# A fused RG-LRU and mixture-of-experts kernel: twelve row tiles for eight, two pairs of PSUM banks for turned tiles, one bank for the second GEMM, and new ranks

## The chip, the cores and the metric

The kernel runs on one core of a Trainium2 chip. The metric is the device time of one execution in microseconds, lower is better. Its engines are TensorE (PE: products; PEld: their weight loads), VectorE (DVE), ScalarE (ACT), GpSimd (POOL) and SyncE (SP), each with its own queue of instructions.

## The reference

A gated linear recurrence runs over four sequences of 5056 tokens with 256 features, and its output goes through a mixture of eight experts, each token to one of them.

```python
log_a = 8.0 * sigmoid(r_gate) * log(clip(sigmoid(a_param), 1e-6, 1 - 1e-6))
a = exp(log_a)
x_gated = sqrt(max(1 - a * a, 1e-6)) * sigmoid(i_gate) * x
for t in range(S):
    h = a[:, t] * h + x_gated[:, t]
    y[:, t] = h
x = y.reshape(20224, 256)
logits = x @ w_gate                           # [N, 8]
e_idx = argmax(logits, axis=1)
gate_w = softmax(logits)[n, e_idx]
eom = sigmoid(x @ w_output_gate)
for e in range(8):
    mask = e_idx == e
    out[mask] = gate_w[mask] * eom[mask, e] * (relu(x[mask] @ w1[e]) @ w2[e])
```

`w1` is [8, 256, 1024], `w2` [8, 1024, 256]. All inputs are float32.

## The kernel before

**Tiles.** The tokens lie along the free axis, features on the partitions. They come in 20 chunks of eight tiles of 128 tokens (the last has six), each chunk in two blocks of 512 tokens. For a block, three loads (L520) bring r, i and x; ScalarE makes tanh, exponential, square and root (L526 to L545), VectorE the gated inputs (L532, L548) and the scan (L579). A block is scaled by a power of two from its maximum (L613, a product on TensorE at L263 that spreads it, L268) and cut into a high and a low half of 16 bits (L627 or L629, L632). Both halves are turned into rows of tokens by products with an identity, which carry the two gates' columns along (L653, "projection", four products of 160 columns into a pair of PSUM banks). ScalarE copies the turned rows into a row tile (L660), VectorE adds the gates' parts up to logits (L664).

**Routing.** When a chunk's eight tiles have logits, VectorE and ScalarE find each token's expert and weight (L673 to L723), TensorE counts places (L694, L696, "ranks"), VectorE makes positions (L727 to L739), and GpSimd scatters the eight row tiles to a table in memory sorted by expert (L354). From chunk 2 on, a scatter also waits for the newest ReLU, so that scatters are spread in time. VectorE then plans slots (L790 to L821): a slot is a run of 256 (early and late in the kernel 128) rows of one expert.

**Slots.** For a slot, SP fetches its rows turned (L868) and the expert's w1 in two halves (L894). GEMM1 (L921) makes hidden units in groups of 512 columns in three PSUM banks; ScalarE's ReLU (L936) and VectorE's rest (L939) split each into two halves of 16 bits. GEMM2 (L965) sums over them, three products for each of eight slices, into one PSUM bank; ScalarE scales it to a result (L977) and GpSimd scatters that to the output (L980). Three slots at the very end run only if they hold rows.

**Weights.** Each of 16 units (eight of w1, eight of w2) is loaded as float32 (L408) into the place of the unit after next, or for the last two into buffers of the slots that chunk 1 has used. A Gram product (L434) and its square (L440) give a power of two, with which it is split (L471 or L473, L481). No slot's weights are fetched before all of w1 is split, no GEMM2 runs before all of w2 is.

**Order.** The program lists all steps as `work(engine, time, emit, after, rank, ...)`, and `in_order` turns the list into one order for each engine: it steps through a modelled time, and each engine that comes free takes, of the steps whose predecessors are done in the model, the one with the least rank. `UNIT_RANK`, `CHUNK_RANK` and `SLOT_RANK` rank units, chunks and the slots of early chunks; later chunks have 2 + c, later slots -5 + s/1000. `TAIL` is added for a chunk's steps from L613 to L664, `ROOT` for its roots, `QUICK` for routing; `EARLY` ranks the projections and ranks on TensorE; `UNIT_LOAD`, `CHUNK_LOAD` and `LOAD_RANK` rank the loads on SP. GEMM2 of a slot has the slot's rank plus `LAG`, GEMM1 the slot's rank plus f/10000 for slice f. The engines then run their instructions in that order, each waiting on semaphores for what it needs.

A `Ring(n)` says in the model when a buffer comes free: a new use waits for the use n before it. The tile pools behind the rings make the same wait on the chip. Of the eight PSUM banks, GEMM1 has three (`ps_h`), GEMM2 and the Gram products two (`ps_o`), projections one pair (`ps_t`), and norms and ranks one (`ps_r`). `rt`, `it` and `xt` hold blocks of r, i and x; a block's buffer of x is in use from its load to its last projection.

Of the kernel before, what the change touches and what calls it, by code (L numbers as in the profile page):

```python
# [7 lines left out]
F32 = mybir.dt.float32  # L8
F16 = mybir.dt.float16
# [3 lines left out]
ALU = mybir.AluOpType  # L13
# [4 lines left out]
P = 128  # L18
# [17 lines left out]
XT = 3  # L36
ROWS = 8
# [4 lines left out]
LAG = 0.05099  # L42
ALONE = (0, 1, 2, 3, 4, 5, 6, 7)
QUICK = 38.13505
ROOT = 275.35116
EARLY = -3648.57348
UNIT_RANK = (56.129, -3501.769, -3458.728, -978.998, -58.723, 38.307, 48.956, 15.508, -257.769, 37.957, -138.469, -385.108, -20.771, -510.085, 59.783, -1.802)
CHUNK_RANK = (-854.714, -3616.617, -3494.371, -1109.025, -778.437, -192.081)
SLOT_RANK = (-1097.603, -1306.253, -459.569, 1089.226)
LOAD_RANK = -3488.5456  # L50
STAGED = {14: ('hh', 'hh'), 15: ('hh', 'ws')}
WINDOW, WARM = 3.413, (0.8, 0.35)
UNIT_LOAD = (244.464, 345.534, 1294.322, -3524.389, -3500.663, -1010.087, 280.646, 98.454, 33.972, -3596.229, 186.523, 60.803, 179.63, -3596.513, -253.138, 1086.46)
CHUNK_LOAD = (84.95, 1021.338, 257.343, 30.647, 1292.223, 0.423)
TAIL = -440.29839
TOPS = 2
TABLES = -854.61171
DEPTH = 3
SLACK = (0.022, 0.414)
# [110 lines left out]
def rglru_moe(ctx: ExitStack, tc: tile.TileContext, x, r_gate, i_gate, a_param, wg, wog, w1, w2, out, shape):  # L170
    nc = tc.nc
    D, N = x.shape
    B, S = shape
    E, _, F = w1.shape
# [6 lines left out]
    while sum(n for _, n in chunks) < NT:  # L181
        t = sum(n for _, n in chunks)
# [29 lines left out]
    ps_o = ctx.enter_context(tc.tile_pool(name="ps_o", bufs=2, space=bass.MemoryType.PSUM))  # L212
    ps_t = ctx.enter_context(tc.tile_pool(name="ps_t", bufs=1, space=bass.MemoryType.PSUM))
    ps_r = ctx.enter_context(tc.tile_pool(name="ps_r", bufs=1, space=bass.MemoryType.PSUM))
# [138 lines left out]
    def scatter_rows(pos, rows, c):  # L353
# [17 lines left out]
        "mt": Ring(6), "ot": Ring(2), "osc": Ring(4), "plan": Ring(3), "ps_h": Ring(3), "ps_o": Ring(2), "am": Ring(4), "ps_t": Ring(1), "ps_r": Ring(1),  # L371
    }
    tiles = {}
# [12 lines left out]
    def unit(u, staged):  # L386
# [10 lines left out]
        m = size // g  # L397
# [27 lines left out]
        pg, old = rings["ps_o"].new()  # L425

        def gram():
            t = tiles["pg", u] = ps_o.tile([P, 512], F32, name=f"pg_{u}", tag="ps_o")
            k = 0
            for fw in fws:  # L430
                upper = fw.bitcast(BF16).rearrange("p (n two) -> p n two", two=2)
                for f in range(0, m, P):
                    blk = upper[:, f:f + P, 1]
                    nc.tensor.matmul(t[:, 0:P], lhsT=blk, rhs=blk, start=k == 0, stop=k == size // P - 1)  # L434
                    k += 1

        def square():
            dg = small.tile([P, P], F32, name=f"dg_{u}", tag="dg", bufs=1)
            sq = tiles["sq", u] = small.tile([P, 1], F32, name=f"sq_{u}", tag="sq")
            nc.scalar.activation(dg, tiles["pg", u][:, 0:P], AF.Square, accum_out=sq)  # L440

        def total():
            nc.tensor.matmul(tiles["pg", u][:, P:P + 1], lhsT=ones32, rhs=tiles["sq", u], start=True, stop=True)
# [53 lines left out]
    def chunk(c):  # L497
# [100 lines left out]
        for b in range(0, nt, 4):  # L598
# [38 lines left out]
            pu, pold = rings["ps_r"].new()  # L637
# [5 lines left out]
            for j in range(b, b + nb):  # L643
# [24 lines left out]
                lows.append(work("DVE", 0.22, lz, [w] + chain["small"], front, uses=[pu]))  # L668
# [76 lines left out]
        pu, pold = rings["ps_r"].new()  # L745
# [26 lines left out]
    def plan(group):  # L772
# [15 lines left out]
        def emit():  # L788
# [4 lines left out]
            nc.vector.tensor_tensor_scan(bound[:, 1:E + 1], ones32[:, 0:E], own, 0.0, op0=ALU.mult, op1=ALU.add)  # L793
# [50 lines left out]
    def slot(s):  # L844
# [63 lines left out]
        for f0 in range(0, NF, per):  # L908
# [33 lines left out]
            m = work("ACT", 0.57, relu, [m, hold], rank, uses=[pu, hu])  # L942
            evac.append(work("DVE", 0.66, low, [m], rank, uses=[pu, hu]))
# [69 lines left out]
    pu, pold = rings["ps_r"].new()  # L1013
# [75 lines left out]
```

## Time and profile before

| | us |
|---|---|
| median of three runs | 1109.23 (1108.28 to 1113.5) |
| the profiled execution | 1111.95 |
| its span, first to last instruction | 1110.3 |
| TensorE busy in the span | 982.2 (88%) |
| VectorE busy | 713.0 (64%) |
| ScalarE busy | 693.4 (62%) |
| GpSimd busy | 354.9 (32%) |
| mean granted clock of TensorE | 0.969 |

Busy time is the union of an engine's instructions. Matmuls are pipelined and overlap, so a busy TensorE is not one at its peak: its work is better counted as products times the distance of their starts. "Idle <- X" means that the engine stood before an instruction and that X ended the wait.

### The profile page before, as it was taken

What the parts mean: (1) busy time and instruction counts of PE and PEld (TensorE: products, weight loads), DVE (VectorE), ACT (ScalarE), POOL (GpSimd) and SP (SyncE); (2) the same over time, 40 slices, a digit from 0 to 9 for tenths busy, and PEclk for the clock granted to TensorE, in tenths of its full rate; (3) what the DMA queues carried; (4) which work ended last, traced back from release to release, by engine and by line L of the source; (5) the groups of instructions that cost most, each with busy time, mean ns of one, the idle gap of its engine ahead of it and who ended that gap; (6) DMA issues with size and microseconds to landing.
All of it is one profiled execution on the core that took longest, in us unless ns stands there. A gap on an engine that the chain in (4) does not pass through costs nothing.

```text
span 1110.3 us, 29698 instructions
## 1 busy us (share of the span) xinstructions
PE 982.2 (88%) x9820; PEld 866.6 (78%) x9820; DVE 713.0 (64%) x1729; ACT 693.4 (62%) x1105; POOL 354.9 (32%) x346
## 2 busy tenths in 40 slices
PE   1355489989999999999989999999999999999997
PEld 1344488878888888788878878888888888888996
DVE  7899878678868667575765657576675753333222
ACT  8995746877786667667666766766676442322222
POOL 1013344243343423324332332433333344312111
PEclk9966599999999999999999999999999999999999
DMA  9972699998867777685968768586875646657782
GB/s 347 387 247 68 215 302 285 300 288 271 248 230 216 234 236 202 211 244 189 239 202 239 199 213 225 208 210 218 258 193 197 192 155 193 173 158 222 240 246 87
DMA packets 196862, 249.42 MB, mean 225 GB/s; under 512 B 120013, under 2 KB 128976, under 8 KB 196720
## 3 DMA queue, kind: packets, MB, share of 16 engines
q1 hardware_dynamic: 180928, 204.17, 62.6%
q0 software_dynamic: 15792, 43.31, 11.7%
q8 instruction: 95, 1.56, 0.6%
q14 instruction: 47, 0.39, 0.1%
HBM read 79.09 MB, written 43.81 MB: 111 GB/s over the span
## 4 chain that ended last, share of the span: by engine, by line
PE 46%; issue 21%; DMA 13%; ACT 8%; DVE 6%; POOL 5%; SPq 1%; POOLq 0%; ACTq 0%; DVEq 0%
PE po L965 21%; PE ph L921 21%; DMA xs<-rows_all,posi 7%; DMA xt<-xs 3%; POOL out_dram L980 3%; PE pt L653 3%; POOL xs L354 2%; ACT rows_all L660 2%; DVE it L579 1%; DMA rt<-in_r_gate_dram 1%; ACT w1r L471 1%; DVE w2r L481 1%; ACT it L540 1%; DMA it<-in_i_gate_dram 1%; ACT it L545 1%
## 5 line engine op out<-in xcount | busy, mean ns | idle before, releaser
L965 PE MATMUL po<-w2r,h 128*128 x3888 | 486.4, 272 | 10.7 <-issue 4.8
L921 PE MATMUL ph<-xt,ws 128*128 128x256 f16 (+1 forms) x4752 | 471.4, 255 | 10.7 <-DMA xt<-xs 5.6
L921 PEld LDWEIGHTS <-ws 128*128 128x128 f16 x4752 | 399.7, 99 | 49.1 <-issue 10.2
L965 PEld LDWEIGHTS <-h 128*128 128x128 f16 x3888 | 373.7, 98 | 72.4 <-issue 16.5
L939 DVE SCALAR_TENSOR_TENSOR h<-ph,h 128x512 f16<-128x512 f32 x324 | 215.0, 684 | 169.0 <-ACT h L936 166.1
L980 POOL DMA_INDIRECT out_dram<-ot,mt x162 | 172.5, 1065 | 386.8 <-ACT ot L977 347.6
L354 POOL DMA_INDIRECT xs<-rows_all,posi x158 | 170.2, 1077 | 352.2 <-issue 159.6
L936 ACT ACTIVATE h<-ph 128x512 f16<-128x512 f32 x324 | 186.1, 599 | 147.9 <-PE po L965 89.2
L660 ACT ACTIVATE rows_all<-pt 128x512 f16<-128x512 f32 x158 | 93.7, 593 | 100.0 <-DMA xs<-rows_all,posi 57.2
L977 ACT ACTIVATE ot<-po,osc 128x256 f32<-128x256 f32 x162 | 70.8, 473 | 121.6 <-PE po L965 104.7
L653 PE MATMUL pt<-iw,xt 128*128 128x160 f16 x632 | 74.8, 243 | 57.6 <-DVE lz L664 33.9
L664 DVE TENSOR_REDUCE lz<-pt 128x16 f32<-128x64 f32 x158 | 35.1, 222 | 122.7 <-PE pt L653 75.6
L653 PEld LDWEIGHTS <-xt 128*128 128x128 f16 x632 | 55.7, 103 | 68.5 <-issue 59.2
L579 DVE TENSOR_TENSOR_SCAN it<-rt,last,it 128x512 f32<-128x512 f32 (+4 forms) x78 | 95.4, 1240 | 0.7
L548 DVE SCALAR_TENSOR_TENSOR it<-it,xt 128x1024 f32<-128x1024 f32 (+1 forms) x40 | 48.3, 1208 | 31.9 <-ACT it L545 31.8
L536 ACT ACTIVATE rt<-rt,lam 128x512 f32<-128x512 f32 (+1 forms) x80 | 61.0, 801 | 0.5
L532 DVE SCALAR_TENSOR_TENSOR xt<-it,xt 128x1024 f32<-128x1024 f32 (+1 forms) x40 | 48.3, 1207 | 6.0 <-ACT it L529 3.2
L632 DVE SCALAR_TENSOR_TENSOR xt<-it,sc,xt 128x1024 f16<-128x1024 f32 (+1 forms) x40 | 49.7, 1265 | 0.3
L613 DVE TENSOR_REDUCE am<-it 128x1 f32<-128x1024 f32 (+1 forms) x40 | 47.8, 1196 | 0.0
L545 ACT ACTIVATE it<-it,quarter 128x1024 f32<-128x1024 f32 (+1 forms) x40 | 45.5, 1138 | 0.4
L529 ACT ACTIVATE it<-it 128x1024 f32<-128x1024 f32 (+1 forms) x40 | 41.6, 1039 | 4.0 <-DMA it<-in_i_gate_dram 3.9
L627 ACT ACTIVATE xt<-it,sc 128x1024 f16<-128x1024 f32 (+1 forms) x36 | 39.8, 1139 | 6.7 <-DVE sc L269 6.7
(146 smaller groups left out, 567.0 us busy)
## 6 DMA issues: line engine op xcount, KB each, us to landing
ws<-w1r SPq DMA_DIRECT2D x198, 512.0 KB
rt<-in_r_gate_dram SPq DMA_DIRECT2D x39, 512.0 KB
it<-in_i_gate_dram SPq DMA_DIRECT2D x39, 512.0 KB
xt<-in_x_dram SPq DMA_DIRECT2D x39, 512.0 KB
w2r<-in_moe_w_dram SPq DMA_DIRECT2D x8, 1024.0 KB
w1r<-in_moe_w_dram SPq DMA_DIRECT2D x6, 1024.0 KB
out_dram<-ot,mt POOLq DMA_INDIRECT x162
xs<-rows_all,posi POOLq DMA_INDIRECT x158
```

The lines of the kernel that those rows point to most:

```text
L354: op = nc.gpsimd.indirect_dma_start(out=xs[:, :], out_offset=bass.IndirectOffsetOnAxis(ap=pos, axis=0), in_=rows.bitcast(F32), in_offset=None,
L536: nc.scalar.activation(r[:, h], r[:, h], AF.Exp, scale=lam[:, h:h + 1], bias=lam[:, h:h + 1])
L545: nc.scalar.activation(t("it"), t("it"), AF.Sqrt, scale=-0.25, bias=quarter)
L579: nc.vector.tensor_tensor_scan(H[:, h, lo:hi], A[:, h, lo:hi], H[:, h, lo:hi], first, op0=ALU.mult, op1=ALU.add)
L653: nc.tensor.matmul(pt[:, k, h * P:h * P + PIECE], lhsT=halves()[:, k, h, (j % 4) * P:(j % 4 + 1) * P], rhs=iw[:, h, :], start=h == 0, stop ...
L660: nc.scalar.activation(rows_all[:, row_at[j], 0:META].rearrange("p (k h d) -> p k h d", k=2, h=ND), src, AF.Copy)
L921: nc.tensor.matmul(ph[:, i], lhsT=ws[:, f // 2 % 2, a, c, f % 2 * P:(f % 2 + 1) * P], rhs=xt[:, b * ND + c, 0:w], start=k == 0, stop=k == ...
L936: newest["relu"] = nc.scalar.activation(part(0, f0), tiles["ph", s, f0], AF.Relu).ins
L939: nc.vector.scalar_tensor_tensor(part(1, f0), tiles["ph", s, f0], 0.0, part(0, f0), op0=ALU.max, op1=ALU.subtract)
L965: nc.tensor.matmul(po[0:pw, j], lhsT=hh[:, a, f % 4, j * P:j * P + pw], rhs=w2r[:, bass.ds(eo + (b * NF + f) * D, D)], start=f + j + a + b ...
L977: nc.scalar.activation(ot[0:pw], tiles["po", s][0:pw, j], AF.Copy, scale=tiles["osc", s][0:pw, j, :])
L980: op = nc.gpsimd.indirect_dma_start(out=out[:, :], out_offset=bass.IndirectOffsetOnAxis(ap=tiles["mt", s][0:pw, j, 1:2].bitcast(I32), axis=0),
```

## The change

Buffers. The ring of row tiles (`rows_all`) has 12 tiles instead of 8. The pool `ps_t` has two pairs of banks instead of one, and norms and ranks use it too, so `ps_r` is gone. `ps_o` has one bank instead of two, and the Gram products use the three banks of `ps_h`. The blocks of gated x (`xt`) have two buffers instead of three. Room for the row tiles comes from these, from `ones16` and `ones32`, which shrink to a column and to eight columns and are broadcast where they are used, and from the dump of the Gram's square, which goes into its own PSUM bank.

Order. All ranks are new, and the modelled times of the logits reduction, ReLU and its rest are smaller. `LAG` goes from 0.051 to 0.001.

```diff
-XT = 3
-ROWS = 8
+XT = 2
+ROWS = 12
...
-LAG = 0.05099
+LAG = 0.00109
...
-QUICK = 38.13505
-ROOT = 275.35116
-EARLY = -3648.57348
-UNIT_RANK = (56.129, -3501.769, -3458.728, -978.998, -58.723, 38.307, 48.956, 15.508, -257.769, 37.957, -138.469, -385.108, -20.771, -510.085, 59.783, -1.802)
-CHUNK_RANK = (-854.714, -3616.617, -3494.371, -1109.025, -778.437, -192.081)
-SLOT_RANK = (-1097.603, -1306.253, -459.569, 1089.226)
-LOAD_RANK = -3488.5456
+QUICK = -11.91443
+ROOT = 992.65936
+EARLY = -2725.80744
+UNIT_RANK = (67.516, 56.172, -366.254, -506.545, 5.629, -24.414, 1010.034, 862.588, -2331.179, -2787.321, 491.753, -2254.652, -778.82, 159.232, -593.189, -2302.865)
+CHUNK_RANK = (-2962.244, -191.208, 477.716, 958.712, 983.504, 13.905)
+SLOT_RANK = (969.557, -4.083, -663.468, -155.487)
+LOAD_RANK = 104.33083
...
-UNIT_LOAD = (244.464, 345.534, 1294.322, -3524.389, -3500.663, -1010.087, 280.646, 98.454, 33.972, -3596.229, 186.523, 60.803, 179.63, -3596.513, -253.138, 1086.46)
-CHUNK_LOAD = (84.95, 1021.338, 257.343, 30.647, 1292.223, 0.423)
-TAIL = -440.29839
+UNIT_LOAD = (239.968, 854.707, -9.185, -227.515, -70.138, 130.966, -238.61, 298.25, -2689.191, 13.907, 336.076, -163.291, 56.472, 348.489, -155.228, 298.416)
+CHUNK_LOAD = (-76.123, 359.624, 952.522, -66.657, -13.306, -105.965)
+TAIL = -2745.68701
...
-TABLES = -854.61171
+TABLES = -315.468
...
-SLACK = (0.022, 0.414)
+SLACK = (0.589, 0.209)
...
-    ps_o = ctx.enter_context(tc.tile_pool(name="ps_o", bufs=2, space=bass.MemoryType.PSUM))
-    ps_t = ctx.enter_context(tc.tile_pool(name="ps_t", bufs=1, space=bass.MemoryType.PSUM))
-    ps_r = ctx.enter_context(tc.tile_pool(name="ps_r", bufs=1, space=bass.MemoryType.PSUM))
+    ps_o = ctx.enter_context(tc.tile_pool(name="ps_o", bufs=1, space=bass.MemoryType.PSUM))
+    ps_t = ctx.enter_context(tc.tile_pool(name="ps_t", bufs=2, space=bass.MemoryType.PSUM))
...
-    ones16 = const.tile([P, P], F16, name="ones16")
+    ones16 = const.tile([P, 1], F16, name="ones16")
...
-    ones32 = const.tile([P, P], F32, name="ones32")
+    ones32 = const.tile([P, E], F32, name="ones32")
...
-        pg, old = rings["ps_o"].new()
+        pg, old = rings["ps_h"].new()
...
-            dg = small.tile([P, P], F32, name=f"dg_{u}", tag="dg", bufs=1)
+            dg = tiles["pg", u][:, 2 * P:3 * P]
...
-                tiles["norm", key] = ps_r.tile([P, 512], F32, name=f"norm_{key[0]}_{key[1]}", tag="ps_r")
+                tiles["norm", key] = ps_t.tile([P, 2, 512], F32, name=f"norm_{key[0]}_{key[1]}", tag="ps_t")[:, 0]
...
-                lows.append(work("DVE", 0.22, lz, [w] + chain["small"], front, uses=[pu]))
+                lows.append(work("DVE", 0.16, lz, [w] + chain["small"], front, uses=[pu]))
...
-            pk = tiles["pk", c] = ps_r.tile([P, 512], F32, name=f"pk_{c}", tag="ps_r")
+            pk = tiles["pk", c] = ps_t.tile([P, 2, 512], F32, name=f"pk_{c}", tag="ps_t")[:, 0]
...
-            m = work("ACT", 0.57, relu, [m, hold], rank, uses=[pu, hu])
-            evac.append(work("DVE", 0.66, low, [m], rank, uses=[pu, hu]))
+            m = work("ACT", 0.48, relu, [m, hold], rank, uses=[pu, hu])
+            evac.append(work("DVE", 0.6, low, [m], rank, uses=[pu, hu]))
```

## Rows read from the trace of the kernel before

**Rows 1.** Windows by stage, from the first GEMM1 to the end. Columns: the stretch, its length, then busy us (number of instructions) of PE, PEld, DVE, ACT and POOL, the granted clock of TensorE, the busy share of the DMA engines, GB/s.

```profile
128.00:250.00 122.00, 110.36 (x1361) 99.03 (x1361) 92.74 (x224) 89.21 (x135) 43.81 (x39) 0.95 1.01 285
250.00:300.00 50.00, 48.68 (x463) 42.56 (x462) 40.85 (x94) 38.29 (x63) 17.84 (x16) 1.00 0.87 260
300.00:890.00 590.00, 559.95 (x5233) 490.16 (x5231) 399.00 (x981) 397.12 (x637) 205.53 (x197) 1.00 0.74 217
890.00:1011.00 121.00, 121.00 (x1186) 107.29 (x1185) 47.10 (x147) 37.91 (x78) 42.81 (x44) 1.00 0.59 174
1011.00:1111.00 100.00, 91.33 (x1180) 83.12 (x1177) 24.85 (x50) 26.49 (x51) 17.72 (x18) 0.98 0.64 198
```

**Rows 2.** Windows of the front, the same columns: two of its three stretches, and the sum of the three (0 to 128 us).

```profile
50.00:100.00 50.00, 28.03 (x249) 25.49 (x248) 46.20 (x90) 44.26 (x71) 12.07 (x8) 0.75 0.62 203
100.00:128.00 28.00, 8.40 (x55) 6.51 (x56) 23.99 (x62) 14.31 (x22) 10.62 (x8) 0.50 0.46 156
sum 128.00, PE 50.85 PEld 44.40 DVE 108.42 ACT 104.34 POOL 27.20; mean PE 16.95 PEld 14.80 DVE 36.14 ACT 34.78 POOL 9.07
```

**Rows 3.** The timelines of TensorE and of ScalarE from 918 to 945 us. Columns: start us, duration us, engine, line, operation, written <- read, how many in a row, and in brackets the idle time before and what ended it. TensorE first.

```profile
920.24 5.40 PE L965 MATMUL po<-w2r,h 128*128 x48
925.48 5.40 PE L921 MATMUL ph<-xt,ws 128*128 128x256 f16 x48
930.72 6.98 PE L965 MATMUL po<-w2r,h 128*128 x60
...
933.59 0.84 ACT L977 ACTIVATE ot<-po,osc 128x256 f32<-128x256 f32 x2 [6.00 <-PE po L965]
```

**Rows 4.** TensorE's groups of instructions by line from 300 to 900 us. Columns: line, operation, names, shapes, how many | busy us, mean ns of one | idle us before them in all, and what ended it.

```profile
L965 PE MATMUL po<-w2r,h 128*128 x2369 | 295.5, 272 | 2.6 <-issue 1.9
L921 PE MATMUL ph<-xt,ws 128*128 128x256 f16 x2398 | 286.8, 272 | 6.4 <-DMA xt<-xs 5.6 <-DVE h L939 0.8
L653 PE MATMUL pt<-iw,xt 128*128 128x160 f16 x404 | 44.3, 232 | 21.0 <-ACT rows_all L660 11.3 <-DVE lz L664 9.7
```

**Rows 5.** What ScalarE waited for from 300 to 900 us, the first row: line <- releaser: us in total, times, longest us.

```profile
ACT rows_all L660 <- DMA xs<-rows_all,posi: 57.2, 30, 3.5
```

**Rows 6.** The timeline of all engines at one chunk's projections, from 556 us on.

```profile
556.22 0.44 PE L653 MATMUL pt<-iw,xt 128*128 128x160 f16 x4 [0.74 <-DVE lz L664]
...
559.59 0.60 ACT L660 ACTIVATE rows_all<-pt 128x512 f16<-128x512 f32 x1 [2.74 <-DMA xs<-rows_all,posi]
...
560.24 0.44 PE L653 MATMUL pt<-iw,xt 128*128 128x160 f16 x4 [1.62 <-ACT rows_all L660]
...
560.71 0.22 DVE L664 TENSOR_REDUCE lz<-pt 128x16 f32<-128x64 f32 x1 [2.60 <-PE pt L653]
```

**Rows 7.** The timelines of GpSimd (575 to 640 us) and ScalarE (583 to 616 us): a scatter of one chunk's rows, and a copy of the next chunk's.

```profile
600.16 1.18 POOL L354 DMA_INDIRECT xs<-rows_all,posi  x1 [0.31 <-issue]
...
605.97 0.60 ACT L660 ACTIVATE rows_all<-pt 128x512 f16<-128x512 f32 x1 [3.34 <-DMA xs<-rows_all,posi]
```

**Rows 8.** The chain that ended last, in order of time, from 575 to 640 us: start us, duration us, what.

```profile
623.81 0.29 PE pt L653 x4
624.12 0.38 SPq L520
...
625.22 6.64 DMA xt<-xs
...
631.99 1.59 PE ph L921 x14
```

**Rows 9.** What SP's queue waited for: the row of the x, r and i loads from 300 to 890 us, then a row of the weight loads over the whole span.

```profile
SPq L520 <- PE pt L653: 55.3, 22, 6.3
...
SPq L408 <- PE pt L653: 12.9, 1, 12.9
```

**Rows 10.** The costliest groups by line of the whole span (the columns of rows 4).

```profile
L579 DVE TENSOR_TENSOR_SCAN it<-rt,last,it 128x512 f32<-128x512 f32 (+4 forms) x78 | 95.4, 1240 | 0.7
...
L532 DVE SCALAR_TENSOR_TENSOR xt<-it,xt 128x1024 f32<-128x1024 f32 (+1 forms) x40 | 48.3, 1207 | 6.0 <-ACT it L529 3.2
L632 DVE SCALAR_TENSOR_TENSOR xt<-it,sc,xt 128x1024 f16<-128x1024 f32 (+1 forms) x40 | 49.7, 1265 | 0.3
...
L545 ACT ACTIVATE it<-it,quarter 128x1024 f32<-128x1024 f32 (+1 forms) x40 | 45.5, 1138 | 0.4
```

**Rows 11.** The timeline of ScalarE in the tail, where slots have 128 rows: one result.

```profile
1059.76 0.47 ACT L977 ACTIVATE ot<-po,osc 128x256 f32<-128x256 f32 x1 [0.71 <-PE po L965]
```

**Rows 12.** TensorE's groups by line with the shapes kept apart: GEMM1.

```profile
L921 PE MATMUL ph<-xt,ws 128*128 128x256 f16 x3024 | 358.5, 272 | 7.2 <-DMA xt<-xs 5.6 <-DVE h L939 1.6
L921 PE MATMUL ph<-xt,ws 128*128 128x128 f16 x1728 | 113.0, 224 | 3.5 <-DMA ws<-w1r 3.2 <-DVE h L939 0.2
```

**Rows 13.** The timelines of TensorE and VectorE at the end of the front: the first products of the slots, and the last split of a weight.

```profile
128.73 0.84 PE L921 MATMUL ph<-xt,ws 128*128 128x128 f16 x6
...
136.98 1.36 PE L965 MATMUL po<-w2r,h 128*128 x9 [1.07 <-ACT h L936]
...
132.32 1.28 DVE L481 SCALAR_TENSOR_TENSOR w2r<-fw,wsc,w2r 128x1024 f16<-128x1024 f32 x1
```

**Rows 14.** The timeline of TensorE's weight loads (PEld) at 10 and 18 us: two with a broadcast operand, two with the full `ones`.

```profile
10.23 0.50 PEld L263 LDWEIGHTS norm_gates<-am_gates 128*128 128x128 f32 x2 [10.23 <-DVE am_gates L993]
...
18.81 0.50 PEld L443 LDWEIGHTS pg<-sq,ones 128*128 128x128 f32 x2 [1.94 <-ACT dg L440]
```

More of the change, by code (lines that the diff above doesn't have):

```diff
@@ L370, in rglru_moe @@
         "rt": Ring(RT), "it": Ring(IT), "xt": Ring(XT), "rows": Ring(ROWS), "ws": Ring(3), "hh": Ring(3), "xt16": Ring(3),
-        "mt": Ring(6), "ot": Ring(2), "osc": Ring(4), "plan": Ring(3), "ps_h": Ring(3), "ps_o": Ring(2), "am": Ring(4), "ps_t": Ring(1), "ps_r": Ring(1),
+        "mt": Ring(6), "ot": Ring(2), "osc": Ring(4), "plan": Ring(3), "ps_h": Ring(3), "ps_o": Ring(1), "am": Ring(4), "ps_t": Ring(2),
     }
@@ L422, in unit @@
         loaded[u] = loads
-        pg, old = rings["ps_o"].new()
+        pg, old = rings["ps_h"].new()
         def gram():
-            t = tiles["pg", u] = ps_o.tile([P, 512], F32, name=f"pg_{u}", tag="ps_o")
+            t = tiles["pg", u] = ps_h.tile([P, 512], F32, name=f"pg_{u}", tag="ps_h")
             k = 0
@@ L442, in total @@
         def total():
-            nc.tensor.matmul(tiles["pg", u][:, P:P + 1], lhsT=ones32, rhs=tiles["sq", u], start=True, stop=True)
+            nc.tensor.matmul(tiles["pg", u][:, P:P + 1], lhsT=ones32[:, 0:1].to_broadcast([P, P]), rhs=tiles["sq", u], start=True, stop=True)
         def bits():
@@ L636, in chunk @@
             w = work("DVE", 0.07 + 1.07 * scale, top, [states[b // 4], aold], front, uses=[iu, au])
-            pu, pold = rings["ps_r"].new()
+            pu, pold = rings["ps_t"].new()
             w = work("PE", 0.15, norm, [w, pold], EARLY + c / 100, uses=[pu, au])
@@ L696, in ranks @@
                 nc.tensor.matmul(
-                    pk[:, k * E:(nt + 1) * E], lhsT=ones16, rhs=o2[:, 0:(nt + 1 - k) * E],
+                    pk[:, k * E:(nt + 1) * E], lhsT=ones16.to_broadcast([P, P]), rhs=o2[:, 0:(nt + 1 - k) * E],
                     start=False, stop=k == nt, skip_group_check=True,
@@ L744, in chunk @@
         cn = work("DVE", 0.9, chosen, [ch, ex], quick)
-        pu, pold = rings["ps_r"].new()
+        pu, pold = rings["ps_t"].new()
         pk = work("PE", 0.35, ranks, [cn, pold], EARLY + c / 100, uses=[pu], slack=SLACK[c > 3])
@@ L792, in emit @@
             nc.vector.tensor_copy(own, li)
-            nc.vector.tensor_tensor_scan(bound[:, 1:E + 1], ones32[:, 0:E], own, 0.0, op0=ALU.mult, op1=ALU.add)
+            nc.vector.tensor_tensor_scan(bound[:, 1:E + 1], ones32, own, 0.0, op0=ALU.mult, op1=ALU.add)
             past, o = tile_of("plt", [GROUP, E + 1])[:, 0:n], tile_of("plo", [GROUP, E], bufs=3)[:, 0:n]
@@ L995, in gate_norm @@
     def gate_norm():
-        tiles["norm", "gates"] = ps_r.tile([P, 512], F32, name="norm_gates", tag="ps_r")
+        tiles["norm", "gates"] = ps_t.tile([P, 2, 512], F32, name="norm_gates", tag="ps_t")[:, 0]
         norm_of(tiles["am", "gates"], "gates")
@@ L1012, in rglru_moe @@
     ld = work("DVE", 4.2, log_decay, [lp], -20)
-    pu, pold = rings["ps_r"].new()
+    pu, pold = rings["ps_t"].new()
     au, aold = rings["am"].new()
```

## The prediction

> **What bounds the kernel now.** I read the windows by stage first [rows 1]. From 128 us to the end TensorE is the bound: 110.4 of 122 us busy, then 48.7 of 50, 560.0 of 590, 121.0 of 121 and 91.3 of 100, with VectorE and ScalarE at 25 to 82%. Before 128 us it is not: TensorE is 50.9 us busy of 128, VectorE 108.4, ScalarE 104.3 [rows 2]. So a saving counts in the front only if the first expert products come earlier, and behind it only if TensorE stands still less.
>
> How dense is TensorE really? In the stretch of nothing but products, 48 of them take 5.24 us from start to start in both GEMMs [rows 3], 0.109 us each at 256 columns. From 300 to 900 us there are 2398 + 2369 of them [rows 4], 520 us; 404 products of projections, of 160 columns, are 28 us at the same rate. Ranks and norms I put at 12. That makes 560 us of work in 600, so 40 us is the most that can be won there. Visible idle time is less, 30.1 us from 300 to 890 [rows 1], because busy spans overlap.
>
> Next the idle time of TensorE from 300 to 900 us by line [rows 4]: 11.3 us of projections (L653) for the ScalarE copy out of their PSUM pair (L660), 9.7 us of projections for the logits reduction (L664), 5.6 us of GEMM1 for gathered rows; the three groups have 30.0 us in all. So 21.0 of 30 us belong to the one pair of banks. Behind it the row copies stood 57.2 us for scatters of earlier rows [rows 5]. The timeline shows the chain: a copy begins at 559.59 after 2.74 us of waiting for a scatter's landing, and the projection behind it begins at 560.24 after 1.62 us of waiting for that copy [rows 6]. One ring of eight row tiles makes a chunk's copy wait for the previous chunk's scatters; one pair makes TensorE wait for the copy.
>
> **The change, part by part.** The sum is made against the profiled execution, 1111.95 us (span 1110.3 and 1.65 around it); the median of the three runs is 2.7 below it.
>
> (1) Two pairs and twelve rows. Projection j then waits for the evacuation of j-2, not j-1. A copy needs 0.60 us and a reduction 0.22, and the two projections stand 4.0 us apart [rows 6], so a free pair should be ready. With twelve row tiles the first four copies of a chunk need none of the previous chunk's scatters, which stand now: a scatter of one chunk begins at 600.16, and a copy of the next chunk, after 3.34 us of waiting for such a landing, at 605.97 [rows 7]. Norms and ranks now take turns in the same two pairs, so some projection will still wait for a DVE read of a norm. Between 0 and -21.0 us; I take -18, near the upper end, since each of these waits [rows 4] names a buffer that the change doubles.
>
> (2) Gathered rows. The chain shows why they are late: a projection ends at 624.1, an x load that waited for its buffer follows on SP, and only behind that is the fetch of a slot issued, whose transpose lands 6.64 us later, at 631.9, where GEMM1 starts [rows 8]. SP's x, r and i loads stood 55.3 us for projections [rows 9]. LOAD_RANK turns from far ahead of the slots (-3488) to behind them (+104), so from chunk 6 on a ready fetch is issued ahead of a load: up to -5.6 us. Against it, XT=2 lets an x load start only after the projection two blocks back, not three; queued behind it on SP are fetches (L868) and weight copies (L894), for which TensorE waits. How late is that? A block's buffer goes through its load (6.6, taken as the fetch of [rows 8]), the gated input (1.2), square and root (1.1 each), the second input (1.2), two scans (2.5), the maximum (1.2), norm and scale (1), the two halves (1.1 and 1.3) and four projections, some 2.5 us apart (10): about 28 us, an estimate from [rows 6, 10], where operations without a row are taken as the nearest of their size. 404 products are 12.6 chunks of 32 in 600 us, 47.5 us for each, so some 20 us of cover are left, and no stall by the mean. Between -5.6 and +20; I take -2.
>
> (3) One bank for GEMM2. Today the next slot's products follow at once in the other bank: the row at 930.72 holds 60 products, and a slot's two results are read at 933.59 for 0.84 us in its middle [rows 3]; 24 products from 930.72 are done by 933.3. With one bank the next product starts after 934.4 at the earliest, 1.2 us later, unless TensorE has something else. For a slot of 128 rows the result takes 0.47 us [rows 11], some 0.75 with its start. The forms give 3024/48 = 63 slots of 256 and 1728/48 = 36 of 128 [rows 12]: 63 x 1.2 + 36 x 0.75 = 103 us if nothing covers it, 0 if all is. The cover is one GEMM1 group of a later slot, 12 x 0.109 = 1.31 us (at 128 rows 24 products of half the width, the same). LAG going from 0.051 to 0.001 ranks GEMM2 of slot s only level with GEMM1 of slot s+1, so GEMM1 no longer runs as far ahead of it as its buffers allow, and the planner knows the ring of one. A group is a little longer than the wait, but where ScalarE is inside an activation of 1.14 us [rows 10] the result comes later. I take a twentieth, +5; ends 0 and +103. From 890 to 1011 us TensorE has no idle time to lose [rows 1], so all of it there would be new.
>
> The trace analysis page of the Trainium skill (Perfetto Trace Analysis, Optimizing Tensor Performance) says that independent groups of products should rotate through banks, so that one is read out while the next is computed. For part (1) the trace agrees, 21.0 us of waits with one pair. For GEMM2 the rule speaks against this change; taken alone it would give the 103 us, and the median would be about 1190.
>
> (4) The front. Units and chunks change their order. Gram products of the weights, the splits and two chunks must be done before slots flow: the first GEMM1 starts at 128.73, the first GEMM2 at 136.98 and the last split at 132.32 [rows 13]. Chunk 2's work (rank -3494 before, 477 now) stood ahead of all units but one. On VectorE it is two blocks of 3 x 1.21 (two inputs and the maximum), two scans of 1.24 and a half of 1.27 [rows 10], 14.8 us, that can now come after some splits. But the last loads of weights were themselves late: they need the buffers of chunk 1, and SP stood 12.9 us for one of its projections [rows 9], and chunk 1 (-3616 before, -191 now) falls behind eight units. Units 6 and 7 of w1, without which no slot starts, come last (1010, 862). Grams move to three GEMM1 banks, which are idle then. The granted clock is 0.75 and 0.50 of 2.4 GHz in the last two stretches of the front [rows 2] and full behind [rows 1]; a front that keeps TensorE busier or less busy shifts that by a few us. Between -15 and +15; I take -3, for VectorE's 19.6 idle us [rows 2] leave room.
>
> (5) The rest. `ones` as broadcast operands: a broadcast weight load already stands in the trace, 0.50 us for two, the same as the full one [rows 14]; 32 and 158 loads, 0. The square's dump into PSUM instead of SBUF, 16 short activations in the front: between -1 and +1, taken as 0. The end: the last two slots have no GEMM1 to put between, so +1.
>
> Sum: -18 - 2 + 5 - 3 + 1 = -17, so 1095 us for a profiled execution and 1092 for the median.
>
> **Rivals.** A, the GEMM2 bank decides (slower). Place: every slot change, above all 890 to 1111 us. Price 103 us times the uncovered share; at a fifth it eats the gain, at two fifths it gives -22 + 41 = +19, 1128 for the median. For it: [rows 3, 11], no idle time today. Against: a GEMM1 group is longer than the read-out. The skill's rule above is this rival; how far the trace bears it out is the wait itself, not its cover.
>
> B, XT=2 chokes SP (slower). Place: x loads L520 with fetches behind them. If each of some 15 chunks pays a third of a landing of 6.64 us, 2.2 us, that is +33 and the gain of (2) is gone: about 1127. For it: the chain of [rows 8] and 55.3 us of SP waits [rows 9]. Against: 20 us of cover.
>
> C, the stall only changes its name. The chain in [rows 7, 8], scatter to landing to copy, or fetch to landing, may recur with each chunk; if it and not the banks sets the pace, GEMM1 waits where projections did, and the time is 1109 +- 5. Against: at 890 us, where the projections are nearly over, 221 us of products remain, so routing is well ahead at the end.
>
> D, all parts win: projections' waits and gathered rows -26, the front -15, no bank wait: 1068.
>
> **How the numbers follow.** Forecast 1082 to 1103.6 (0.50), D (0.12), C (0.15), A (0.14), B (0.09). The predicted time is 1092. What a measurement can tell from no change is about 0.5%, 5.5 us. Faster by more: forecast and D, 0.62. Within: C and a little of A and B, 0.16. Slower: A and B, 0.22. The range 1070 to 1120 leaves out the far half of A and B and a little beyond D.
>
> **What would show it.** (1) right: TensorE's waits at L653 from 300 to 900 us fall under 5 us and ScalarE's at L660 for scatters under 20. (2): GEMM1 waits for gathered rows stay under 6 us. (3) right: waits of L965 for L977 under 10 us in all; A: over 25. (4): first GEMM2 between 122 and 152 us. C: L653's waits fall, L921's for gathered rows rise by as much. I am wrong if TensorE's idle time after 300 us is not smaller than the 38.7 us of now (30.0 and 8.7, [rows 1]).

## The result, and the profile after

The changed kernel takes 1079.64 us (median of four runs, 1072.69 to 1080.02) against 1108.76 for the kernel before in the same set: a ratio of 0.9717, 95% interval 0.9667 to 0.9768. A second set gave 0.9705 (0.9683 to 0.9726). The forecast was 1092, so sign and range were right and the gain was 29 us where I had 17; the median lies below the stretch of the forecast (1082 to 1103.6) and above rival D (1068). The profiled execution took 1080.02 us (span 1078.3), 31.9 less than the one of before. Line numbers of the new kernel are one lower: L652 is the projection, L659 the row copy, L663 the logits, L920 GEMM1, L964 GEMM2, L976 the result. Runs made from the kernel before keep its numbers.

First the windows by stage of the changed kernel, columns as in [rows 1].

```profile
128.00:250.00 122.00, 109.98 (x1367) 97.99 (x1365) 95.82 (x244) 88.52 (x140) 47.78 (x40) 0.96 1.01 290
250.00:300.00 50.00, 47.30 (x435) 41.51 (x433) 40.06 (x101) 38.20 (x59) 19.77 (x18) 0.97 0.85 245
300.00:890.00 590.00, 583.26 (x5499) 515.96 (x5497) 412.10 (x1020) 404.15 (x656) 238.94 (x217) 1.00 0.74 228
890.00:1011.00 121.00, 121.00 (x1297) 109.79 (x1295) 41.03 (x110) 36.81 (x70) 23.61 (x24) 1.00 0.56 178
1011.00:1111.00 100.00, 61.27 (x807) 56.83 (x804) 17.18 (x35) 17.77 (x35) 12.78 (x13) 0.98 0.39 132
```

TensorE stands still for 6.7 us from 300 to 890 us, 30.1 before; in the two stretches ahead of that, 14.7 where it was 13.0. Now its groups by line from 300 to 900 us, the same view as [rows 4].

```profile
L964 PE MATMUL po<-w2r,h 128*128 x2507 | 334.8, 272 | 3.4 <-ACT ot L976 2.9
L920 PE MATMUL ph<-xt,ws 128*128 128x256 f16 x2508 | 329.2, 272 | 0.0
L652 PE MATMUL pt<-iw,xt 128*128 128x160 f16 x408 | 38.4, 232 | 2.3 <-ACT rows_all L659 1.3 <-DVE lz L663 0.9
```

The counts say more than the busy time, since spans overlap: 2507 + 2508 products against 2369 + 2398, 248 more in the same 600 us. At 0.109 us each [rows 3] that is 27.0 of the 32.0 us by which the span shrank. At 300 us the two kernels are level: the view by line from 0 to 300 us, with GEMM1's shapes kept apart, has the same 816 narrow products in both, and 582 + 224 wide ones against 576 + 233. The last 5 us came after 900 us; 2.0 of them are visible idle time of the last stretch (99.3 - 91.33 before, 67.3 - 61.27 now), of the rest I have no account.

What TensorE waited for over the whole span, line <- releaser: us in total, times, longest us; the bank of GEMM2 first in the fence, then the two projection waits that [rows 4] showed.

```profile
PE po L964 <- ACT ot L976: 7.3, 12, 1.6
PE pt L652 <- DVE lz L663: 6.0, 2, 5.1
...
PE pt L652 <- ACT rows_all L659: 3.3, 7, 1.5
```

ScalarE's copies no longer wait for any scatter between 300 and 900 us (57.2 us in [rows 5]).

How the one bank of GEMM2 is covered shows in the timelines around one change of slots, first TensorE, then ScalarE (columns as in [rows 3]).

```profile
900.27 0.82 PE L920 MATMUL ph<-xt,ws 128*128 128x256 f16 x6
900.93 0.82 PE L964 MATMUL po<-w2r,h 128*128 x6
901.59 1.47 PE L920 MATMUL ph<-xt,ws 128*128 128x256 f16 x12
902.89 1.55 PE L964 MATMUL po<-w2r,h 128*128 x12
```

```profile
901.84 0.84 ACT L976 ACTIVATE ot<-po,osc 128x256 f32<-128x256 f32 x2
```

GEMM2 of one slot ends with the six products of 900.93. ScalarE reads the result from 901.84 to 902.68, and TensorE has twelve products of GEMM1 in that time, so the next slot's GEMM2 starts at 902.89 without waiting. In the kernel before, 48 products of one GEMM stood in a row [rows 3]; now GEMM1 and GEMM2 alternate by sixes.

Last, VectorE's timeline where a chunk's last logits (`lz`, L663) are made, routing starts (`mx`, L672) and positions are ready (`posi`, L733). The changed kernel first, then the kernel before (L664, L673, L734).

```profile
587.23 0.22 DVE L663 TENSOR_REDUCE lz<-pt 128x16 f32<-128x64 f32 x1 [0.30 <-PE pt L652]
587.48 0.22 DVE L672 TENSOR_REDUCE mx<-lz 128x8 f32<-128x64 f32 x1
...
594.10 0.22 DVE L733 TENSOR_REDUCE posi<-pos 128x8 int32<-128x64 f32 x1
```

```profile
574.84 0.22 DVE L664 TENSOR_REDUCE lz<-pt 128x16 f32<-128x64 f32 x1
...
585.24 0.21 DVE L673 TENSOR_REDUCE mx<-lz 128x8 f32<-128x64 f32 x1
...
593.68 0.22 DVE L734 TENSOR_REDUCE posi<-pos 128x8 int32<-128x64 f32 x1
```

In these rows of before, routing begins 10.4 us after the last logits and the positions come 18.8 us after them; in those of after 0.25 and 6.9. The other chunks go the same way: over chunks 7 to 18, a chunk's first scatter begins 18.5 us after its last logits in the median before, and 8.3 after. The rank that speaks of this is `QUICK`: 2 + c + 38 ranked routing of chunk c behind the gating and the scans of every chunk, 2 + c - 11.9 ranks it ahead of them and, from chunk 6 on, behind the steps of the slots (-5 + s/1000). My prediction has no term for it.

### The profile page after: what moved, and what is told of

It is laid out like the page before. It is cut to its first block, busy times and chain, and to the rows that moved or that the text cites. A ratio compares the mean times of both kernels' runs of the same rounds, so it can differ in the third digit from the quotient of the medians.

```text
span 1078.3 us, 29704 instructions
## 1 busy us (share of the span) xinstructions
PE 972.3 (90%) x9820; PEld 866.3 (80%) x9820; DVE 715.3 (66%) x1743; ACT 687.5 (64%) x1101; POOL 372.8 (35%) x346
## 4 chain that ended last, share of the span: by engine, by line
PE 54%; DMA 8%; ACT 8%; issue 7%; DVE 7%; POOL 3%; SPq 2%; POOLq 0%; ACTq 0%; DVEq 0%
PE po L964 27%; PE ph L920 25%; DMA xt<-in_x_dram 3%; POOL xs L353 2%; PE pt L652 2%; ACT rows_all L659 2%; DMA ws<-w1r 1%; DVE h L938 1%; ACT h L935 1%; DMA rt<-in_r_gate_dram 1%; POOL out_dram L979 1%; DMA xs<-rows_all,posi 1%; DVE it L578 1%; SPq L867 1%; ACT ot L976 1%
## 5 line engine op out<-in xcount | busy, mean ns | idle before, releaser
L964 PE MATMUL po<-w2r,h 128*128 x3888 | 534.0, 273 | 11.5 <-ACT ot L976 7.3
L920 PE MATMUL ph<-xt,ws 128*128 128x256 f16 (+1 forms) x4752 | 528.2, 255 | 15.6 <-DMA xt<-xs 9.2
L920 PEld LDWEIGHTS <-ws 128*128 128x128 f16 x4752 | 409.6, 99 | 56.2 <-issue 12.6
L964 PEld LDWEIGHTS <-h 128*128 128x128 f16 x3888 | 372.2, 98 | 64.6 <-issue 12.9
L935 ACT ACTIVATE h<-ph 128x512 f16<-128x512 f32 x324 | 190.7, 597 | 292.2 <-PE ph L920 287.1
L938 DVE SCALAR_TENSOR_TENSOR h<-ph,h 128x512 f16<-128x512 f32 x324 | 219.7, 686 | 222.4 <-ACT h L935 222.0
L353 POOL DMA_INDIRECT xs<-rows_all,posi x158 | 185.8, 1176 | 311.3 <-ACT h L935 134.3
L659 ACT ACTIVATE rows_all<-pt 128x512 f16<-128x512 f32 x158 | 88.3, 595 | 31.5 <-PE pt L652 16.6
L652 PE MATMUL pt<-iw,xt 128*128 128x160 f16 x632 | 66.0, 243 | 22.3 <-ACT xt L626 8.9
L976 ACT ACTIVATE ot<-po,osc 128x256 f32<-128x256 f32 x162 | 69.8, 470 | 8.0 <-PE po L964 4.9
L652 PEld LDWEIGHTS <-xt 128*128 128x128 f16 x632 | 51.6, 102 | 27.5 <-issue 11.6
L531 DVE SCALAR_TENSOR_TENSOR xt<-it,xt 128x1024 f32<-128x1024 f32 (+1 forms) x40 | 48.3, 1209 | 16.2 <-DMA xt<-in_x_dram 12.8
L663 DVE TENSOR_REDUCE lz<-pt 128x16 f32<-128x64 f32 x158 | 31.6, 220 | 40.7 <-ACT rows_all L659 27.7
L525 ACT ACTIVATE rt<-rt 128x1024 f32<-128x1024 f32 (+1 forms) x40 | 41.8, 1046 | 13.5 <-DMA rt<-in_r_gate_dram 13.3
L539 ACT ACTIVATE it<-rt 128x1024 f32<-128x1024 f32 (+1 forms) x40 | 41.8, 1045 | 8.7 <-DVE xt L531 7.0
```

Of the source, the lines that this page charges most:

```text
L353: op = nc.gpsimd.indirect_dma_start(out=xs[:, :], out_offset=bass.IndirectOffsetOnAxis(ap=pos, axis=0), in_=rows.bitcast(F32), in_offset=None,
L652: nc.tensor.matmul(pt[:, k, h * P:h * P + PIECE], lhsT=halves()[:, k, h, (j % 4) * P:(j % 4 + 1) * P], rhs=iw[:, h, :], start=h == 0, stop ...
L659: nc.scalar.activation(rows_all[:, row_at[j], 0:META].rearrange("p (k h d) -> p k h d", k=2, h=ND), src, AF.Copy)
L920: nc.tensor.matmul(ph[:, i], lhsT=ws[:, f // 2 % 2, a, c, f % 2 * P:(f % 2 + 1) * P], rhs=xt[:, b * ND + c, 0:w], start=k == 0, stop=k == ...
L935: newest["relu"] = nc.scalar.activation(part(0, f0), tiles["ph", s, f0], AF.Relu).ins
L938: nc.vector.scalar_tensor_tensor(part(1, f0), tiles["ph", s, f0], 0.0, part(0, f0), op0=ALU.max, op1=ALU.subtract)
```

## The experiments

Theory 1 is the prediction's: the waits of [rows 4, 5] go because buffers are doubled. Theory 2 says that they go because routing starts at once, so that row tiles are given back early. Each ratio is to the kernel before, run beside it on the same chip, with its 95% interval. From set to set that kernel's median lay between 1108.76 and 1121.72 us, so ratios are compared here, not times.

**All new ranks, old buffers.** The kernel before with every rank, `LAG`, `SLACK` and modelled time of the changed one.

```diff
-LAG = 0.05099
+LAG = 0.00109
...
-QUICK = 38.13505
+QUICK = -11.91443
...
```

> The kernel before with all new ranks, LAG, SLACK and modelled times, but its old buffers (8 row tiles, one pair of banks for projections, two banks for GEMM2, three blocks of gated x). Theory 1, the buffers make the gain: 1098 to 1112 us, TensorE's waits at the projection line from 300 to 900 us stay over 12 us. Theory 2, the order makes the gain: 1076 to 1090 us, those waits under 8 us.

Measured: 0.9914 (0.9881 to 0.9946). From 300 to 900 us the projections wait 8.4 + 3.4 us instead of 21.0, and the copies 3.4 us for scatters instead of 57.2. So the order alone takes off nearly half of the first and nearly all of the second; as a ratio to 1108.76 us, the time is in theory 1's range (0.990 to 1.003), and the waits lie between the marks of the two, 12 and 8 us. But the new order needs the second pair in the beginning, as the windows show:

```profile
250.00:300.00 50.00, 38.33 (x340) 32.98 (x340) 38.17 (x92) 40.36 (x60) 16.53 (x16) 0.83 0.72 212
```

TensorE has 38.3 of 50 us there, 48.7 in [rows 1]. Its timeline has projections one after the other on the single pair, with no GEMM between them:

```profile
252.05 0.69 PE L653 MATMUL pt<-iw,xt 128*128 128x160 f16 x4 [3.96 <-ACT rows_all L660]
255.94 0.69 PE L653 MATMUL pt<-iw,xt 128*128 128x160 f16 x4 [3.20 <-ACT rows_all L660]
```

**New buffers, old ranks.** The reverse: the changed kernel with the ranks, `LAG`, `SLACK` and modelled times of before.

```diff
-LAG = 0.00109
+LAG = 0.05099
...
-QUICK = -11.91443
+QUICK = 38.13505
...
```

> The changed kernel with all old ranks, LAG, SLACK and modelled times, and its new buffers. Theory 1 (buffers): 1076 to 1092 us, waits of TensorE at the projection line from 300 to 900 us under 6 us. Theory 2 (order): 1098 to 1112 us. Rival A on the single GEMM2 bank: with LAG 0.051 the waits of GEMM2 for its result copies rise over 15 us.

Measured: 1.0718 (1.0684 to 1.0753), 1202 us, slower than either theory allowed. GEMM2 waits 54.2 us for its bank over the whole span (rival A's mark was 15), and from 128 to 250 us TensorE is busy for 78.7 of 122 us, 110.4 before. Under an order made for other buffers the new ones cost time, above all the one bank. What the longer ring and the second pair are worth under the old order, this run can't tell.

**Eight row tiles** in the changed kernel.

```diff
-ROWS = 12
+ROWS = 8
```

> The changed kernel with a ring of 8 row tiles again, planned anew for it. If the row ring carries the gain (a copy stands for a scatter, and a projection for the copy): 1092 to 1105 us and ScalarE's waits for scatters at the copy line from 300 to 900 us over 30 us. If the second pair of banks carries it: 1080 to 1088 us, TensorE's projection waits still under 6 us while ScalarE stands for scatters.

Measured: 0.9744 (0.9711 to 0.9778), 0.3 to 0.4% above the two ratios of the changed kernel, with intervals that overlap. With eight tiles the copies still wait for no scatter from 300 to 900 us. The trace of the changed kernel says the same of its twelve: none of the 102 copies from 300 to 900 us begins before GpSimd issues the scatter of the tile eight copies earlier, and all but two begin 4 us or more after that. With early routing the larger ring is hardly used.

**Old PSUM pools** in the changed kernel: one pair, a bank for norms and ranks, two for GEMM2; twelve rows, two blocks and the new ranks stay.

```diff
-    ps_o = ctx.enter_context(tc.tile_pool(name="ps_o", bufs=1, space=bass.MemoryType.PSUM))
-    ps_t = ctx.enter_context(tc.tile_pool(name="ps_t", bufs=2, space=bass.MemoryType.PSUM))
+    ps_o = ctx.enter_context(tc.tile_pool(name="ps_o", bufs=2, space=bass.MemoryType.PSUM))
+    ps_t = ctx.enter_context(tc.tile_pool(name="ps_t", bufs=1, space=bass.MemoryType.PSUM))
+    ps_r = ctx.enter_context(tc.tile_pool(name="ps_r", bufs=1, space=bass.MemoryType.PSUM))
...
```

> The changed kernel with the old split of PSUM: one pair of banks for projections, one bank for norms and ranks, two for GEMM2; 12 row tiles and all ranks as changed. If the second pair carries the gain: 1092 to 1105 us, projection waits of TensorE over 12 us from 300 to 900 us. If the row ring carries it: 1078 to 1088 us, projection waits under 8 us. GEMM2 should wait for its result copies under 3 us in all (7.3 us with one bank).

Measured: 0.9849 (0.9822 to 0.9876). GEMM2 has no listed wait for a bank, and projections wait 5.0 + 2.4 us from 300 to 900 us. The loss is early again: 36.1 of 50 us busy from 250 to 300 us. So with this order the new split of PSUM, a second pair in place of the second bank of GEMM2 and the bank of norms and ranks, is worth some 1.4%, most of it before 300 us, where the prediction had placed its gain behind 300.

**The changed kernel again**, for a second ratio beside the next three.

> The changed kernel itself, beside the kernels of this call on one chip. All theories: 0.972 of the kernel before, with projection waits of TensorE near 2 us from 300 to 900 us.

Measured: 0.9705 (0.9683 to 0.9726). Projections wait 0.3 us for copies from 300 to 900 us, and GEMM2 11.1 us for its bank over the whole span.

**The old `LAG`** for slots of the chunks from 4 on, in the changed kernel: GEMM1 of the next slot is again ranked ahead of GEMM2, on one bank.

```diff
-            m = work("PE", 0.327 * q, multiply2, [m, evac[f // per], ready] + (every if f == 0 else []), rank + LAG + f / 1e4, uses=[pu, hus[f // 4][0], vuse])
+            m = work("PE", 0.327 * q, multiply2, [m, evac[f // per], ready] + (every if f == 0 else []), rank + (LAG if c < 4 else 0.05099) + f / 1e4, uses=[pu, hus[f // 4][0], vuse])
```

> The changed kernel with LAG 0.051 for the slots of chunk 4 and later, so that their first GEMM runs ahead as far as its buffers allow; one bank for GEMM2 as changed. Rival A's mechanism (a bank's read-out is covered only while a group of GEMM1 is left to put between): GEMM2's waits for its result copies from 300 to 900 us rise from 2.9 to over 20 us and the time by 15 to 60 us. If the bank never matters: waits under 8 us, time within 6 us of the changed kernel.

Measured: 1.0338 (1.0319 to 1.0357), 71 us above the changed kernel on the same chip; I had expected 60 at most. TensorE's timeline and then ScalarE's, at a change of slots:

```profile
960.89 0.82 PE L964 MATMUL po<-w2r,h 128*128 x6
962.69 3.19 PE L964 MATMUL po<-w2r,h 128*128 x24 [0.98 <-ACT ot L976]
```

```profile
961.80 0.84 ACT L976 ACTIVATE ot<-po,osc 128x256 f32<-128x256 f32 x2 [4.20 <-issue]
```

Here GEMM2 of the next slot follows at once. Six products take 0.66 us, so it could start at 961.55 and starts at 962.69: 1.14 us lost, the 1.2 us that part (3) had worked out. The waits for the bank are 47.6 us in the whole span, 11.1 in the repeat above. That is about half of the 71 us; a listed wait is a little shorter than the loss (0.98 us here for 1.14), and for the rest I have no account.

**Three blocks of gated input, eight row tiles** in the changed kernel, to be held against eight tiles with two blocks.

```diff
-XT = 2
-ROWS = 12
+XT = 3
+ROWS = 8
```

> The changed kernel with three blocks of gated x and 8 row tiles, against the one with two blocks and 8 row tiles (0.9744 of the kernel before). If two blocks cost nothing, as the 20 us of cover say: 0.970 to 0.979. If x loads that wait for projections cost time: 0.955 to 0.967, and SP's waits of x, r and i loads for projections fall by half.

Measured: 0.9794 (0.9767 to 0.9820), against 0.9744 with two. The third block brings nothing. SP's loads wait 36.0 us for projections from 300 to 890 us with it, 32.5 without.

**One rank in the kernel before.** Routing of the chunks from 6 on gets the changed kernel's `QUICK`; buffers and all other ranks stay.

```diff
-        quick = rank + QUICK
+        quick = rank + (QUICK if c < 6 else -11.91443)
```

> The kernel before with one rank changed: QUICK -11.9 instead of 38.1 for chunks 6 and later, so that their routing goes ahead of the next chunk's gating; all buffers and the front's order as before. If the slow routing sets when row tiles come free: ScalarE's waits for scatters fall from 57.2 us to under 20, TensorE's projection waits from 300 to 900 us from 21.0 to 8 to 14 us, time 0.985 to 0.993. If the ring of 8 sets it: waits over 40 us, time 0.996 to 1.004.

Measured: 0.9741 (0.9723 to 0.9759), a larger gain than I had expected (0.985 at best). TensorE's groups from 300 to 900 us, to be held against [rows 4]:

```profile
L965 PE MATMUL po<-w2r,h 128*128 x2496 | 303.8, 272 | 3.5 <-issue 3.2 <-DVE it L579 0.2
L921 PE MATMUL ph<-xt,ws 128*128 128x256 f16 x2471 | 291.8, 272 | 2.6 <-DVE h L939 2.5
L653 PE MATMUL pt<-iw,xt 128*128 128x160 f16 x408 | 44.8, 232 | 3.1 <-ACT rows_all L660 2.9
```

With one pair and eight row tiles, projections wait 3.1 us instead of 21.0, and GEMM1 waits for no gathered rows. The row of ScalarE's waits that stood at 57.2 us in [rows 5] is now:

```profile
ACT rows_all L660 <- DMA xs<-rows_all,posi: 8.9, 6, 3.6
```

A chunk's first scatter begins 12.6 us after its last logits in the median over chunks 7 to 18, 18.5 before. So no buffer was needed to remove this stall. It was a late start of routing, seen from the far end of a chain of buffers.

**The old `QUICK` in the changed kernel**, for the same chunks.

```diff
-        quick = rank + QUICK
+        quick = rank + (QUICK if c < 6 else 38.13505)
```

> The changed kernel with QUICK 38.1 again for chunks 6 and later, everything else as changed (12 row tiles, two pairs, one GEMM2 bank). Theory 2, early routing makes the gain of the long stretch: 0.983 to 0.995 of the kernel before, GEMM1's waits for gathered rows or projection waits from 300 to 900 us back over 8 us. Theory 1, the buffers can stand in for early routing: 0.968 to 0.977, those waits under 4 us each, no wait of ScalarE for scatters over 10 us.

Measured: 0.9813 (0.9777 to 0.9850). Projections wait 0.9 + 1.8 us from 300 to 900 us and the copies 4.8 for scatters. But the old rank doesn't make routing begin late in this kernel, since a rank only decides among steps that are ready. The timelines of VectorE, GpSimd and ScalarE around one chunk show its last logits, routing (`mx`), positions and weights (L721), then its first and its seventh scatter, then the next chunk's seventh copy:

```profile
570.18 0.36 DVE L663 TENSOR_REDUCE lz<-pt 128x16 f32<-128x64 f32 x2 [0.59 <-ACT rows_all L659]
...
570.58 0.21 DVE L672 TENSOR_REDUCE mx<-lz 128x8 f32<-128x64 f32 x1
...
578.45 0.22 DVE L733 TENSOR_REDUCE posi<-pos 128x8 int32<-128x64 f32 x1
...
597.82 0.18 DVE L721 RECIPROCAL rows_all<-sm 128x4 f32<-128x4 f32 x1
```

```profile
599.63 0.96 POOL L353 DMA_INDIRECT xs<-rows_all,posi  x1 [2.24 <-ACT h L935]
...
620.66 0.96 POOL L353 DMA_INDIRECT xs<-rows_all,posi  x1 [1.83 <-ACT h L935]
```

```profile
613.47 0.60 ACT L659 ACTIVATE rows_all<-pt 128x512 f16<-128x512 f32 x1 [0.25 <-PE pt L652]
```

Routing begins at once and the positions come 8 us after the logits, but the weights only at 597.82 and the first scatter 29 us after the logits. Over chunks 7 to 18 that is 19.6 us in the median, as late as before (18.5). Here the longer ring is used: the copy of 613.47 begins 7.2 us before the scatter of the tile eight copies earlier, and 37 of the 102 copies from 300 to 900 us begin before theirs. So row tiles that come back late stop nothing in this kernel, and with eight of them those copies would have had to wait. Neither theory's numbers fit in full: theory 1 holds for the waits and theory 2 has the last 1% of time. What the other new ranks do to the waits here is not separated from the buffers. GEMM2's waits for its bank are 9.1 us from 300 to 900 us, 2.9 in the changed kernel.

**`LOAD_RANK` alone in the kernel before**, part (2) of the prediction by itself.

```diff
-LOAD_RANK = -3488.5456
+LOAD_RANK = 104.33083
```

> The kernel before with LOAD_RANK +104 instead of -3488 alone (loads of chunks 6 and later behind the slots' fetches on SP). If loads ahead of fetches cost the 5.6 us of GEMM1's waits for gathered rows: those waits under 2 us, time 0.993 to 0.997, projection waits unchanged near 21 us. If the late routing makes them: waits stay over 4 us, time 0.997 to 1.004.

Measured: 1.0000 (0.9981 to 1.0019). What TensorE waited for from 300 to 900 us (us in total, times, longest us):

```profile
PE pt L653 <- ACT rows_all L660: 8.6, 12, 1.8
PE ph L921 <- DMA xt<-xs: 7.2, 1, 7.2
PE ph L921 <- DMA mt<-xs: 7.0, 1, 7.0
...
PE pt L653 <- DVE lz L664: 1.9, 1, 1.9
```

Against what I had expected, the projections' waits halve, from 21.0 to 10.5 us, and the copies wait 33.7 us for scatters instead of 57.2. But GEMM1 waits once for 7.2 us for gathered rows and once for 7.0 us for a slot's table of tokens, which is read from the same scattered rows (`mt`), where the kernel before has 5.6 us in six short waits. TensorE stands still for 28.1 us in all from 300 to 900 us, 30.0 before: here the stall changed its name, as rival C has it. Scatters are late as before, 21.4 us after the last logits in the median.

**`QUICK` and `LOAD_RANK` in the kernel before**, both edits together.

```diff
-LOAD_RANK = -3488.5456
+LOAD_RANK = 104.33083
...
-        quick = rank + QUICK
+        quick = rank + (QUICK if c < 6 else -11.91443)
```

> The kernel before with both QUICK -11.9 for chunks 6 and later and LOAD_RANK +104, old buffers. If the two ranks together make the whole change: 0.966 to 0.973. If LOAD_RANK adds nothing to QUICK: 0.972 to 0.977, as with QUICK alone.

Measured: 0.9888 (0.9860 to 0.9915), where `QUICK` alone gave 0.9741. That is outside both ranges. With the old buffers the later loads cost 1.5%; projections wait 6.2 us for logits and the copies 20.9 for scatters. Why is open.

**Routing ahead of everything** in the changed kernel: `QUICK` -400 for the chunks from 6 on, so ahead of the slots too.

```diff
-        quick = rank + QUICK
+        quick = rank + (QUICK if c < 6 else -400.0)
```

> The changed kernel with QUICK -400 for chunks 6 and later, so that routing goes ahead of the slots' own steps too. If latency of routing still costs: 0.960 to 0.968. If the long stretch is down to what is left of TensorE's own work (6.7 us of idle time from 300 to 890 us): 0.968 to 0.975.

Measured: 1.0787 (1.0745 to 1.0828). That is far outside both ranges: earlier isn't better without end. From 300 to 890 us TensorE is busy for 502.6 of 590 us; the timeline of TensorE at one such place, and ScalarE's:

```profile
460.70 1.44 PE L964 MATMUL po<-w2r,h 128*128 x6 [3.28 <-ACT ot L976]
```

```profile
459.15 1.13 ACT L626 ACTIVATE xt<-it,sc 128x1024 f16<-128x1024 f32 x1
460.19 0.45 ACT L976 ACTIVATE ot<-po,osc 128x256 f32<-128x256 f32 x1
```

The result's read-out stands behind chunk work on ScalarE, and the one bank makes TensorE wait for it, 44.7 us in all from 300 to 900 us. That is half of the 87 us for which TensorE stands still from 300 to 890 us; its granted clock is 0.92 there, 1.00 in the changed kernel.

## Why the prediction was right, and where it was not

**The main claim held.** TensorE was the bound behind 128 us, and the time went where it stood idle. Of the 40 us that I had read from the counts as the most to be won from 300 to 900 us, 27 were. By the same working (5015 x 0.109 + 408 x 28/404 + 12) 587 of 600 us are work now. The named tests came out so: projections' waits 2.3 us (under 5), copies' waits for scatters 0 (under 20), gathered rows 0.0 (under 6), GEMM2's bank 7.3 (under 10; 11.1 in the repeat), first GEMM2 at 134.94 (between 122 and 152), TensorE's idle time after 300 us 12.8 within the span (38.0 before). Rival C fell for the changed kernel with the third of these: the waits did not reappear under another name, as they did with `LOAD_RANK` alone.

**(1) Two pairs and twelve rows, -18.** The waits went from 21.0 to 2.3 us, but the reason given, "each of these waits names a buffer that the change doubles", was only half of it. The row names who is waited for, not why that one is late. The kernel before with one changed rank has 3.1 us of these waits with no buffer doubled; the changed kernel with the old `QUICK` has 2.7 of them. Either kernel is rid of them, and the two don't add up: 1.000 with neither, 0.974 with early routing, 0.981 with the buffers and the other ranks, 0.971 with all. In the changed kernel itself the second pair is in use, since 66 of the 102 projections from 300 to 900 us begin before the one ahead is evacuated, but the four more row tiles are not needed there, so that half of the argument was right for another kernel than the one that was built. This is where the missing size lies. What comes nearest to the prediction's argument, waits removed by buffers, is the kernel with the old `QUICK`, where the longer ring is in use, although the other new ranks are in it too: -21 us (1091.84 against 1113.16), where the sum had -17. The new `QUICK` adds some 1% to that, 11 us, and for this the sum had no term, though the rank stood in the diff.

**(2) Gathered rows, -2.** The wait of 5.6 us went, but not by `LOAD_RANK`: alone it gave 1.000 and 14.2 us of such waits. In the kernel with early routing alone no such wait is left: the fetches were late because routing was. `XT` = 2 costs nothing, as taken (0.9744 with two, 0.9794 with three, both with eight row tiles); rival B is out.

**(3) One bank for GEMM2, +5.** The waits rose from the 2.9 us of before to 7.3, +4.4. The cover was the one named, a GEMM1 group of twelve products during the read-out, and `LAG` makes it. Without it the price is real: 71 us with the old `LAG`, about half of it in listed waits, of 103 worked out for no cover at all. Rival A was a true mechanism with nearly the right price per slot (1.14 us measured, 1.2 worked out; the times it was worked out from, 933.3 and 934.4, give 1.1), and the order kept it off.

The Trainium skill's rule of rotating banks (Perfetto Trace Analysis, Optimizing Tensor Performance) says that independent groups go through different banks, so that one is read out while the next is computed. The kernel with the old `LAG` agrees, 47.6 us of waits. The changed kernel, 7.3 us, does not go against it: the products in GEMM2's read-out are those of GEMM1, in other banks, and the prediction had applied the rule to GEMM2 alone.

**(4) The front, -3.** The first GEMM1 starts at 124.89 instead of 128.73 and the first GEMM2 at 134.94 instead of 136.98 [rows 13]. That is given back: from 250 to 300 us TensorE has 47.3 us instead of 48.7, and at 300 us the counts are level. So 0, and the bounds of 15 to either side were far too wide. What each rank of the front is worth alone was not tried; the two kernels that had the new ranks and one pair of banks show that the new order has a price of its own: 11.7 and 13.9 us of idle time from 250 to 300 us, where the kernel before has 1.3.

**(5) The rest, +1.** After 900 us the changed kernel gained 5 us instead. 2.0 are idle time; what makes the rest stays open.

Left open as well: what the other new ranks did to the waits without the buffers and without the new `QUICK`, and why `LOAD_RANK` costs 1.5% beside early routing on the old buffers. Three blocks beside twelve rows was not tried. No kernel of these runs beats the changed one; the kernel before with one changed rank comes within 0.4% of it.

## What to carry to other kernels

When an engine waits for a buffer, follow the buffer to the step that gives it back last, and look when that step began: here one rank on the old buffers gave 0.974, the new buffers with the other ranks 0.981, and all together only 0.971. Look in the trace, too, whether a rank moved its step at all: the same old `QUICK` held routing back by some 10 us in one order and not in the other. Count the instructions per stretch and multiply by their distance from start to start: 248 more products in 600 us settled 27 of 32 us, where idle time showed 23. A single bank is cheap only as long as the order puts other products into its read-out; whoever shrinks a pool must ask which order goes with it (0.97 with the new one, 1.07 with the old).

## What was not expected of the hardware

TensorE loses nothing by changing between two accumulations every six products: the sixes of 900.27, 900.93 and 901.59 are 0.66 us apart, 0.109 us a product, the same as in rows of 48 [rows 3]. And the same kernel differed by 1.2% between sets of runs, 1108.76 to 1121.72 us in the median: more than the 0.4% between the two best versions here, so that times of different sets say nothing about them.
